# State attention and a Mish layer: the first batch's state read moved, one product widened, the start's list written anew

## The chip, the core and the metric

The kernel runs on one core of a Trainium2 chip. The metric is the device time of one execution in microseconds (us). TensorE is called PE below (its weight loads PEld), VectorE DVE, ScalarE ACT, GpSimd POOL; SP is SyncE, which here only issues DMAs. A kernel's time is the median of its runs; one further run was taken with the profiler.

## The reference

```python
def _attn_ref(x, state):            # x (8, 8, 512, 64), state (8, 8, 32, 64)
    scores = scale * np.matmul(x, state.transpose(0, 1, 3, 2))
    ...                             # softmax over the last axis: a
    xread = np.matmul(a, state)
    scores2 = scale * np.matmul(state, x.transpose(0, 1, 3, 2))
    ...                             # softmax over the last axis: a2
    sread = np.matmul(a2, x)
    return np.concatenate([xread, sread], axis=2).astype(np.float32)

def _moe_ref(x, w_in, w_out):       # w_in (512, 2048), w_out (2048, 512), 64-bit floats
    h = x @ w_in
    sp = np.where(h > 20.0, h, np.log1p(np.exp(np.minimum(h, 20.0))))
    g = h * np.tanh(sp)
    return (g @ w_out).astype(np.float32)
```

The 8 heads of 64 are laid side by side, so each of the 8 batches gives 512 tokens from `xread` and 32 from `sread`, all of width 512, and these go through the second function.

## The kernel before

**Tokens of x.** For the tokens of `xread`, the kernel doesn't form `a @ state` but `ph = a (state w_in)`: `swp` is the small product of a batch's state (block by block, `bd`) with a slice of `w_in`, and `ph` that of the softmax weights with it. Then g = Mish(ph) and `acc` += g w_out. A precise product takes three fast ones of high and low parts: `ah swh`, `al swh`, `ah swl` for `ph`, and likewise `gh`, `gl` with the two parts of `wo` for `acc`. The work goes in 8 groups j of 256 columns of `w_in`: gemm1 makes `ph` in two banks, gemm2 adds to the four banks of `acc` (one for each 128 tokens).

**State tokens.** They need `sread` of a batch: the transposed softmax weights `e2T` times x give `srp`, scaled into `srd`. Its transpose in high and low parts is `srT`; it has room for all 8 batches, 256 tokens. These go through gemm1_s (`ph_s`) and gemm2 (`acc_s`) once, ahead of batch 7.

**The start.** Weights arrive as 64-bit words in 8 pieces of `w_in` (`wir`) and 8 of `w_out` (`wor`). Each is scaled (steps h), rounded (c on ACT, d on DVE) and joined (j) to 32-bit floats; w_out then gets its parts (`wh`, `lo`). This and the whole of batch 0 run by a list of step names (lines 803 to 814). `InOrder` (line 58) keeps DVE and ACT to the order of the list and PE and the loads to that of the program. Capital letters are steps of batch 1, whose softmax is done in the same list.

**The rest.** After the list, loops over the batches (`key` 1 to 7) and j (0 to 7) write the steps, and the scheduler orders DVE and ACT. The product `second` of a group stands one or two groups behind its `first`. All DMAs but two are issued by SP, in one order.

**What the change touches.** Of batch 0's state read, the list has: `mm` and `ee` (softmax over the tokens), `et` (`e2_transposed`, line 393: PE transposes `e` into `e2p`, ACT copies it to `e2T`), `sr` (`sread`, line 494) and `rt` (`sreadT`, line 513: one PE transpose `srTp`, then two parts). In later batches `e2_turned` (line 380) takes the place of `et`: DVE transposes blocks of 32 into `u`, and 16 DMAs put them in order in `e2T`; `soft2` (the softmax) and this step, `turn`, of batch 1 stand at key 1, j = 0 and 1. x_0 lies in the place of the last piece of `w_out`, `wo7`. gemm1_s stands at line 620. The loads are written in one line ahead of the list (line 697).

Of the kernel before, what the change touches and what calls it, by code (L numbers as in the profile page):

```python
# [17 lines left out]
P = 128  # L18
# [59 lines left out]
def state_attention_mish_kernel(ctx, tc, x, state, w_in, w_out, out):  # L78
# [39 lines left out]
    srT = [const.tile([P, NC, B * NS], F32R, name=f"srT_{n}") for n in ("h", "l")]  # L118

    def load_x(b):  # L120

        shape = [P, NC, 2, NT * D]
        if b == 0:
            xs = const.tile(shape, F32, tag="wo7", name="x_0")
        else:
            xs = pool.tile(shape, F32, tag="x", name=f"x_{b}", bufs=1)
        for c in range(NC):
            last["load"] = nc.sync.dma_start(
                xs[:, c], x[b].rearrange("(c k) (p t) d -> c p k (t d)", k=2, t=NT)[c])
        return xs  # L130
# [152 lines left out]
    def attention(b, sn, xq=None):  # L283
# [16 lines left out]
        def scores_q():  # L300

            pss = [bank(f"sc_{b}_{q}") for q, bank in enumerate((misc, misc, first_bank, first_bank))]
            order = [(k, i, c) for k in range(2) for i in range(2) for c in range(NC)]
            if b == 0:
                order.sort(key=lambda s: s[2])
            for k, i, c in order:
                o = slice(c * NS, (c + 1) * NS)
                for q in range(4):
                    last["PE"] = pe.matmul(
                        pss[q][o, k * P:(k + 1) * P].rearrange("n (t p) -> n t p", t=NT),  # L310
                        bqs[b][quad(q), i, 2 * c + k],
                        xTs[c][quad(q)].rearrange("d (k t i p) -> d k i t p", k=2, t=NT, i=2)[:, k, i],
                        start=(i == 0), stop=(i == 1))
            yield
            scs = pool.tile([P, 2, S], F32, tag="sc", name=f"scs_{b}", bufs=1)
# [64 lines left out]
        def e2_turned():  # L380

            both = pool.tile([P, 2 * NT, P], F32, tag="e2T", name=f"e2T_{b}", bufs=1)
            for kc in range(2):
                e2T[kc] = both[:, kc * NT:(kc + 1) * NT]
            u = pool.tile([P, 2, S], F32, tag="sc", name=f"u_{b}", bufs=1)
            for kc in range(2):
                dve.transpose(u[:, kc], e2s[kc])
            v = u.rearrange("i k (t q n) -> i q (k t) n", t=NT, q=4)
            for c in range(NC):
                for q in range(4):  # L390
                    nc.sync.dma_start(both[quad(q), :, quad(c)], v[quad(c), q])

        def e2_transposed(kc):
            e2 = e2s[kc]
            pt = misc(f"e2p_{b}_{kc}")
            for t in range(NT):
                pe.transpose(pt[:, t * P:(t + 1) * P], e2[:, t * P:(t + 1) * P], ident)
            yield
            if not e2T:
                both = pool.tile([P, 2 * NT, P], F32, tag="e2T", name=f"e2T_{b}", bufs=1)  # L400
                e2T.update({k: both[:, k * NT:(k + 1) * NT] for k in range(2)})
            act.copy(e2T[kc].rearrange("p t n -> p (t n)"), pt)


# [89 lines left out]
        def sread(kc):  # L494

            if b == 0 or kc == 0:
                srd["bank"] = misc(f"srp_{b}_{kc}") if b == 0 else spare(2)(f"srp_{b}")
            pr = srd["bank"][:, :D] if b == 0 else srd["bank"][:, kc * D:(kc + 1) * D]
            for t in range(NT):
                for h4 in range(4):  # L500
# [3 lines left out]
                        e2T[kc][:, t, o],  # L504
# [4 lines left out]
            if kc == 0 and b == 0:  # L509
                srd[0] = pool.tile([P, 2, D], F32, tag="srd", name=f"srd_{b}", bufs=1)  # L510
            dve.tensor_scalar_mul((srds[0][:, b - 1] if b else srd[0])[:, kc], pr, rs2[kc])

        def sreadT():
            pt = misc(f"srTp_{b}")[:, :P]
            pe.transpose(pt, srd[0].rearrange("p k d -> p (k d)"), ident)
            yield
            ptv = pt.rearrange("p (c n) -> p c n", c=NC)
            hi, lo = (t[..., b * NS:(b + 1) * NS] for t in srT)
            act.copy(hi, ptv)
            yield  # L520
            dve.tensor_sub(lo, ptv, as_f32(hi))

        own = dict(
            x=x_transposed, st=lambda _: state_blocks(b, sn) if b else state_blocks_0(sn), sc=lambda _: scores() if b > 1 else scores_q(), tr=soft1_t, ex=soft1_x,
            no=lambda _: soft1_n(), pr=soft1_a, mm=soft2_m, ee=soft2_e, et=e2_transposed, sr=sread,
            rt=lambda _: sreadT(), fill=fill, aT=aT)
# [12 lines left out]
    def sreads_transposed():  # L539
        for bs in (range(1, 5), range(5, B)):  # L540
            pt = first_bank(f"srTp_{bs[0]}")
            for i, b in enumerate(bs):
                pe.transpose(pt[:, i * P:(i + 1) * P], srds[0][:, b - 1].rearrange("p k d -> p (k d)"), ident)
# [45 lines left out]
    def low_g(g, gh, gl):  # L589
        dve.tensor_sub(gl, g, as_f32(gh))  # L590
# [132 lines left out]
    def mish_half(j, k):  # L723
# [5 lines left out]
        dve.tensor_copy(gh[:, k * 512:(k + 1) * 512], g[:, k * 512:(k + 1) * 512])  # L729
# [9 lines left out]
    def high_w_half(o, k):  # L739
        if o not in wo:  # L740
            new_wo(o)
        dve.tensor_copy(wo[o][:, k, 1], wfull[o][:, k])
# [15 lines left out]
    def by_tiles(j):  # L758
# [5 lines left out]
    at0, at1 = attention(0, sn0), attention(1, sn1)  # L764
# [22 lines left out]
        "ga": lambda j: by_tiles_half(j, 0), "gb": lambda j: by_tiles_half(j, 1),  # L787
        "wha": lambda o: high_w_half(o, 0), "whb": lambda o: high_w_half(o, 1),
# [6 lines left out]
        "fill": lambda i: at0["fill"](i, accs[0][NT - 1]), "acc": lambda _: new_accs(0, NT),  # L795
        "next": lambda _: sw_slice(1, 0),
# [41 lines left out]
    srds[0] = pool.tile([P, B - 1, 2, D], F32, tag="wt", name="srds", bufs=1)  # L838
    for key, j in slots:
# [24 lines left out]
        if key == 1 and j == 0:  # L864
            prev["soft2"]()
# [35 lines left out]
        if more and j == 4:  # L901
            with behind("swh", "swl"):
# [45 lines left out]
```

## Time and profile before

| | us |
|---|---|
| median of 3 runs | 650.08 |
| lowest and highest | 649.78, 650.28 |
| the profiled run | 649.78 |
| its span | 648.0 |
| PE busy | 640.3 (99%) |
| DVE busy | 353.0 (54%) |
| ACT busy | 246.9 (38%) |

The span goes from the first to the last thing that the profiler recorded. In the profile every computing instruction has line 70, since `InOrder` issues them all; so rows are told apart by the names of their tiles (`out<-in`). A row of the timeline has the start, the time until the last of its instructions ended, the engine, the operation and the count; as products overlap in the pipeline, their pace is read from one row's start to the next one's.

### The profile page before, as it was taken

How to read it: one execution, taken by the hardware profiler on the slowest of the kernel's cores; microseconds unless marked ns; L12 is line 12 of the kernel's file. 1: busy time of each engine (PE TensorE's matmuls, PEld its weight loads, DVE VectorE, ACT ScalarE, POOL GpSimd, SP SyncE). 2: the span in 40 equal slices, each digit the busy share in tenths (PEclk: the TensorE clock that was granted, in tenths of full speed). 3: DMA queues.
4: the chain of work that ended last, by engine and by line, in shares of the span. 5: the costliest groups of instructions: out<-in, count | busy, mean ns of one | idle time of the engine just before them, and what ended most of it. 6: DMA issues, size and time to landing. Idle time of an engine off the chain costs nothing.

```text
span 648.0 us, 11382 instructions
## 1 busy us (share of the span) xinstructions
PE 640.3 (99%) x4686; PEld 515.9 (80%) x4686; DVE 353.0 (54%) x551; ACT 246.9 (38%) x395; POOL 0.7 (0%) x6
## 2 busy tenths in 40 slices
PE   8899999999999999999999999999999999999997
PEld 6677777787878888787878788787878799878886
DVE  5999994674529363655338262855359254332222
ACT  4987952452226122532226212622236234131110
POOL 0000000000000000000000000000000000000000
PEclk9999999999999999999999999999999999999999
DMA  8986323430134103420234003410112001000001
GB/s 322 411 276 207 47 43 81 105 50 5 45 67 109 19 9 92 104 34 9 71 60 93 8 8 98 107 26 1 66 66 34 1 1 66 1 17 17 1 0 66
DMA packets 112611, 46.04 MB, mean 71 GB/s; under 512 B 93744, under 2 KB 102192, under 8 KB 112560
## 3 DMA queue, kind: packets, MB, share of 16 engines
q1 hardware_dynamic: 112128, 45.12, 26.0%
q8 instruction: 37, 0.61, 0.4%
q10 hardware_dynamic: 432, 0.20, 0.1%
q14 instruction: 14, 0.11, 0.1%
HBM read 32.70 MB, written 8.91 MB: 64 GB/s over the span
## 4 chain that ended last, share of the span: by engine, by line
PE 96%; DMA 2%; ACT 1%; DVE 0%; issue 0%; SPq 0%
PE acc L70 55%; PE ph L70 27%; PE swp L70 5%; PE ph_s L70 4%; PE acc_s L70 3%; DMA wor<-in_moe_w_out_dram 1%; PE srp L70 1%; PE sc L70 1%; DMA x<-in_x_dram 0%; DVE s L70 0%; DVE e L70 0%; ACT L70 0%; ACT wor L70 0%; ACT ah L70 0%; ACT wir L70 0%; PE e2p L70 0%
## 5 line engine op out<-in xcount | busy, mean ns | idle before, releaser
L70 PE MATMUL acc<-wo,gh 128*128 128x512 f32 x1024 | 318.4, 392 | 0.0
L70 PEld LDWEIGHTS acc<-wo,gh 128*128 128x128 f32 x1024 | 190.4, 188 | 46.6 <-issue 7.2
L70 PE MATMUL acc<-wo,gl 128*128 128x512 f32 x512 | 199.4, 389 | 0.0
L70 ACT ACTIVATE g<-ph 128x512 f32<-128x512 f32 x128 | 73.7, 597 | 226.2 <-DVE gl L70 207.0
L70 DVE CAST gh<-g 128x1024 fp32r<-128x1024 f32 (+1 forms) x61 | 41.5, 680 | 134.0 <-PE acc L70 132.1
L70 PEld LDWEIGHTS acc<-wo,gl 128*128 128x128 f32 x512 | 96.1, 188 | 20.4
L70 DVE TENSOR_TENSOR gl<-g,gh 128x1024 fp32r<-128x1024 f32 (+1 forms) x65 | 78.3, 1205 | 4.5
L70 PE MATMUL ph<-ah,swh 128*128 128x512 f32 x256 | 79.4, 392 | 0.2 <-ACT g L70 0.2
L70 PE MATMUL ph<-ah,swl 128*128 128x512 f32 x256 | 78.9, 390 | 0.0
L70 PE MATMUL ph<-al,swh 128*128 128x512 f32 x256 | 78.8, 390 | 0.0
L70 DVE TENSOR_TENSOR swl<-swp,swh 128x512 fp32r<-128x512 f32 (+1 forms) x72 | 41.0, 624 | 48.0 <-ACT swh L70 48.0
L70 ACT ACT_TABLE_LOAD x35 | 44.9, 1283 | 31.1 <-DVE s L70 13.5
L70 PEld LDWEIGHTS ph<-ah,swh 128*128 128x128 f32 x256 | 47.5, 188 | 11.3 <-ACT g L70 0.8
L70 PEld LDWEIGHTS ph<-ah,swl 128*128 128x128 f32 x256 | 48.1, 188 | 10.4 <-DVE swl L70 0.4
L70 PEld LDWEIGHTS ph<-al,swh 128*128 128x128 f32 x256 | 48.0, 188 | 10.4 <-DVE al L70 0.4
L70 ACT CAST swh<-swp 128x512 fp32r<-128x512 f32 (+1 forms) x72 | 34.6, 546 | 29.8 <-PE swp L70 29.7
L70 PE MATMUL swp<-w_in_sb,bd 64*32 64x256 f32 x1024 | 34.9, 381 | 0.0
L70 PEld LDWEIGHTS swp<-w_in_sb,bd 64*32 64x32 f32 x1024 | 19.0, 106 | 11.8 <-issue 5.3
L70 DVE COPY o<-acc 128x512 f32<-128x512 f32 x16 | 11.0, 691 | 31.0 <-PE acc L70 31.0
L70 ACT COPY o<-acc 128x512 f32<-128x512 f32 (+1 forms) x17 | 9.5, 563 | 44.1 <-PE acc L70 44.1
L70 DVE STREAM_TRANSPOSE xT<-xq 128x512 f32<-128x512 f32 x24 | 23.7, 1063 | 0.0
L70 PE MATMUL acc_s<-wo,gh_s 128*128 128x512 f32 x64 | 20.0, 394 | 0.0
(90 smaller groups left out, 453.8 us busy)
## 6 DMA issues: line engine op xcount, KB each, us to landing
x<-in_x_dram SPq DMA_DIRECT2D x32, 256.0 KB, 3.7
wir<-in_moe_w_in_dram SPq DMA_DIRECT2D x16, 512.0 KB, 10.0
wor<-in_moe_w_out_dram SPq DMA_DIRECT2D x16, 512.0 KB, 8.0
xq<-in_x_dram SPq DMA_DIRECT2D x192, 32.0 KB, 2.3
out_dram<-o SPq DMA_DIRECT2D x23, 256.0 KB, 2.4
e2T<-u SPq DMA_DIRECT2D x112, 32.0 KB, 1.9
out_dram<-o SPq DMA_DIRECT2D x32, 64.0 KB, 1.7
sn<-in_state_dram SPq DMA_DIRECT2D x28, 32.0 KB, 2.1
```

Of the source, the lines that this page charges most:

```text
L70: made = method(*args, **kwargs)
```

## The change

1. Batch 0's state read leaves the list. The weights `e` are turned at the list's end by the later batches' step (`tu`: two DVE transposes into `u`, 16 DMAs into `e2T`), x_0 is loaded a second time, and `sread` stands at key 1, j = 1. `sreadT` and `e2_transposed` go; the transposes of the state tokens have all 8 batches. Batch 1's `soft2` and `turn` stand one group later.
2. `e2T` and `u` have another layout, so that each transfer moves 32 rows in pieces of 256 numbers rather than of 32.
3. gemm1_s takes both parts of `srT` in one product of 512 columns with the weights' high part, and one of 256 with their low part; the two halves are added by DVE before Mish.
4. The loads become steps of the list (`ldi`, `ldo`, `lx`), the list is written anew, and some copies can be made by ACT (`Ma`, `Mb`, `Wa`, `Wb`).
5. `soft1` of the later batches gets one more rule of order ("low before").

```diff
-    srT = [const.tile([P, NC, B * NS], F32R, name=f"srT_{n}") for n in ("h", "l")]
+    srT_both = const.tile([P, NC, 2, B * NS], F32R, name="srT")
+    srT = [srT_both[:, :, i] for i in range(2)]
...
-            both = pool.tile([P, 2 * NT, P], F32, tag="e2T", name=f"e2T_{b}", bufs=1)
+            both = pool.tile([P, NC, 2, NT, NS], F32, tag="e2T", name=f"e2T_{b}", bufs=1)
             for kc in range(2):
-                e2T[kc] = both[:, kc * NT:(kc + 1) * NT]
-            u = pool.tile([P, 2, S], F32, tag="sc", name=f"u_{b}", bufs=1)
+                e2T[kc] = both[:, :, kc]
+            u = pool.tile([P, 4, 2, NT * NS], F32, tag="sc" if b else "wt", name=f"u_{b}", bufs=1)
             for kc in range(2):
-                dve.transpose(u[:, kc], e2s[kc])
-            v = u.rearrange("i k (t q n) -> i q (k t) n", t=NT, q=4)
+                dve.transpose(
+                    u[:, :, kc].rearrange("i q (t n) -> i t q n", t=NT),
+                    e2s[kc].rearrange("n (t q p) -> n t q p", t=NT, q=4))
             for c in range(NC):
                 for q in range(4):
-                    nc.sync.dma_start(both[quad(q), :, quad(c)], v[quad(c), q])
+                    nc.sync.dma_start(
+                        both[quad(q), c].rearrange("p k t n -> p (k t n)"), u[quad(c), q].rearrange("i k m -> i (k m)"))
...
-        def sreadT():
...
-        for bs in (range(1, 5), range(5, B)):
+        for bs in (range(4), range(4, B)):
...
     def gemm1_s(j):
 
         g = new_g(f"s_{j}")
-        ph = [ps_h.tile([P, 512], F32, tag="ph", name=f"ph_s_{j}_{r}") for r in range(2)]
         for r in range(2):
             for k in range(2):
                 fc = 4 * j + 2 * r + k
+                ph = (first_bank, misc)[k](f"ph_s_{j}_{r}_{k}")
...
                 for c in range(NC):
-                    for n, (l, i) in enumerate(((hi, 0), (hi, 1), (lo, 0))):
-                        pe.matmul(
-                            ph[r][:, k * 256:(k + 1) * 256], l[:, c], srT[i][:, c],
-                            start=(c == 0 and n == 0), stop=(c == NC - 1 and n == 2))
-        for r in range(2):
-            take_g(g, r, ph[r])
+                    pe.matmul(
+                        ph, hi[:, c], srT_both[:, c].rearrange("p i t -> p (i t)"),
+                        start=(c == 0), stop=(c == NC - 1))
+                for c in range(NC):
+                    pe.matmul(
+                        ph[:, :256], lo[:, c], srT[0][:, c], start=False, stop=(c == NC - 1), skip_group_check=True)
+                to = g[:, (2 * r + k) * 256:(2 * r + k + 1) * 256]
+                act.copy(to, ph[:, 256:])
+                dve.tensor_add(to, to, ph[:, :256])
+                last["mish"] = act.activation(to, to, AF.Mish)
...
-    load(("i", 0), ("o", 0), ("i", 1), ("i", 2), ("o", 1), ("i", 3), ("o", 2), ("i", 4), ("o", 3), ("i", 5))
-    with behind("load"):
-        xss[1], sn1 = load_x(1), load_state(1)
-    load(("o", 4), ("o", 6), ("o", 5), ("i", 6), ("i", 7), ("o", 7))
...
-            st acc st x0 hia0 x1 st x2 x3 dia0 jia0 sc sc sc sc tr0 sc tr1 coa0 dib0 fill2 tr0
...
+            st st x1 x0 ldi0 ldo0 hia0 x2 acc ldi1 ldi2 x3 st sc ldo1 fill2 dia0 ldo3 sc ldi3 jia0 sc tr0 ldo2
...
+            ja7 g5 n6 PR0 ja7 lg6 PR1 p7 PR1 PR0 next g6 g6 next g6 lo7 PR1 g6 PR0 next tu n7 n7 lg7
...
+    xss[0] = pool.tile([P, NC, 2, NT * D], F32, tag="raw", name="x_0_again", bufs=2)
+    with behind("load"):
+        load_x(0, xss[0])
...
-        if key == 1 and j == 0:
-            prev["soft2"]()
...
         if key == 1 and j == 1:
-            with behind("mish"):
-                prev["turn"]()
+            beside += [at0["sr"](k) for k in range(2)]
...
+        if key == 1 and j == 1:
+            with behind("swl"):
+                prev["soft2"]()
+        if key == 1 and j == 2:
+            with behind("mish"):
+                prev["turn"]()
```

How the instructions stand at three places, by the order in which each engine gets them. A row has the line, the operation, the tiles written and read, a shape and a count; numbers in a name tell batch, group or part, a last number only one tile from another.

**SP, from the last load of a weight to the first results.** Before:

```order
L191 DMA wor_153<-in_moe_w_out_dram 128x1024 x2
L224 DMA sn_1130<-in_state_dram 32x8x32 x4
L141 DMA xq_1097<-in_x_dram 32x8x32 x32
L391 DMA e2T_1222<-u_1223 32x8x32 x16
L684 DMA out_dram<-o_0_1179 32x512 x4
L684 DMA out_dram<-o_1_1191 32x512 x4
```

After:

```order
L182 DMA wir_400<-in_moe_w_in_dram 128x2x512 x2
L227 DMA sn_1095<-in_state_dram 32x8x32 x4
L144 DMA xq_1062<-in_x_dram 32x8x32 x32
L131 DMA x_again<-in_x_dram 128x2x256 x4
L395 DMA e2T_1035<-u_1036 32x256 x16
L671 DMA out_dram<-o_0_1132 32x512 x4
L671 DMA out_dram<-o_1_1144 32x512 x4
L227 DMA sn_1835<-in_state_dram 32x8x32 x4
L671 DMA out_dram<-o_2_1243 32x512 x4
L671 DMA out_dram<-o_3_1255 32x512 x4
L395 DMA e2T_1326<-u_1327 32x256 x16
```

Before, the first 16 `e2T` are batch 1's and stand ahead of batch 0's results; now those in this place are batch 0's, behind the second load of x_0, and batch 1's follow the four stores of results.

**PE, around batch 0's `srp`.** Before, in the list, between groups 3 and 2:

```order
L70 MATMUL ph_3_1_574<-al_344,swh_3_562 128x512 x2
L70 MATMUL ph_3_1_574<-ah_343,swl_3_563 128x512 x2
L70 MATMUL e2p_1_589<-ident,e_0_1_519 128x128 x4
L70 MATMUL srp_0_605<-x_79,e2T_570 32x64 x16
L70 MATMUL acc_0_179<-wo_546,gh_2_596 128x512 x2
```

After, in batch 1 (`acc` with `gh_7` is batch 0's last group, `ph_2` batch 1's third):

```order
L70 MATMUL swp_2_0_1175<-w_in_sb,bd_604 32x256
L70 MATMUL swp_2_1_1176<-w_in_sb,bd_604 32x256
L70 MATMUL srp_1193<-x_again,e2T_1035 32x64 x32
L70 MATMUL acc_2_132<-wo_961,gh_7_1058 128x512 x2
L70 MATMUL acc_2_132<-wo_961,gl_7_1059 128x512
```

Both halves of `srp` (16 rows each) now stand together, behind a slice of `swp`, and `e2p` is gone.

**PE, the first block of the state tokens.** Before, three such rows stand four times for each block; here are the last three of the first block and the first three of the second:

```order
L70 MATMUL ph_s_0_5113<-srT_h,wh_0_0_5115 128x256
L70 MATMUL ph_s_0_5113<-srT_l,wh_0_0_5115 128x256
L70 MATMUL ph_s_0_5113<-srT_h,wl_0_0_5116 128x256
L70 MATMUL ph_s_0_5113<-srT_h,wh_0_1_5131 128x256
L70 MATMUL ph_s_0_5113<-srT_l,wh_0_1_5131 128x256
L70 MATMUL ph_s_0_5113<-srT_h,wl_0_1_5132 128x256
```

After, the first two blocks whole, behind the last row of batch 6 ahead of them:

```order
L70 MATMUL acc_3_4588<-wo_918,gl_6_4949 128x512
L70 MATMUL ph_s_0_0_5119<-srT,wh_0_0_5120 128x512 x4
L70 MATMUL ph_s_0_0_5119<-srT,wl_0_0_5121 128x256 x4
L70 MATMUL ph_s_0_1_5135<-srT,wh_0_1_5136 128x512 x4
L70 MATMUL ph_s_0_1_5135<-srT,wl_0_1_5137 128x256 x4
```

Products with `srT_h` and `srT_l` by the same weights became one, and each block has a bank of its own.

More of the change, by code (lines that the diff above doesn't have):

```diff
@@ L116, in state_attention_mish_kernel, with load_x @@
     wo = {}
-    srT = [const.tile([P, NC, B * NS], F32R, name=f"srT_{n}") for n in ("h", "l")]
-    def load_x(b):
+    srT_both = const.tile([P, NC, 2, B * NS], F32R, name="srT")
+    srT = [srT_both[:, :, i] for i in range(2)]
+    def load_x(b, xs=None):
         shape = [P, NC, 2, NT * D]
-        if b == 0:
+        if xs is not None:
+            pass
+        elif b == 0:
             xs = const.tile(shape, F32, tag="wo7", name="x_0")
@@ L314, in scores_q @@
             yield
-            scs = pool.tile([P, 2, S], F32, tag="sc", name=f"scs_{b}", bufs=1)
+            scs = pool.tile([P, 2, S], F32, tag="sc" if b else "e2T", name=f"scs_{b}", bufs=1)
             for kc in range(2):
@@ L494, in sread @@
         def sread(kc):
-            if b == 0 or kc == 0:
-                srd["bank"] = misc(f"srp_{b}_{kc}") if b == 0 else spare(2)(f"srp_{b}")
-            pr = srd["bank"][:, :D] if b == 0 else srd["bank"][:, kc * D:(kc + 1) * D]
+            if kc == 0:
+                srd["bank"] = first_bank(f"srp_{b}")
+            pr = srd["bank"][:, kc * D:(kc + 1) * D]
             for t in range(NT):
@@ L503, in sread @@
                         pr[o],
-                        e2T[kc][:, t, o],
+                        e2T[kc][:, h4, t],
                         xss[b][:, h4, kc, t * D:(t + 1) * D],
@@ L508, in sread @@
             yield
-            if kc == 0 and b == 0:
-                srd[0] = pool.tile([P, 2, D], F32, tag="srd", name=f"srd_{b}", bufs=1)
-            dve.tensor_scalar_mul((srds[0][:, b - 1] if b else srd[0])[:, kc], pr, rs2[kc])
-        def sreadT():
[L514 to L521, printed above, removed]
+            if not srds:
+                srds[0] = pool.tile([P, B, 2, D], F32, tag="wt", name="srds", bufs=1)
+            dve.tensor_scalar_mul(srds[0][:, b, kc], pr, rs2[kc])
         own = dict(
-            x=x_transposed, st=lambda _: state_blocks(b, sn) if b else state_blocks_0(sn), sc=lambda _: scores() if b > 1 else scores_q(), tr=soft1_t, ex=soft1_x,
-            no=lambda _: soft1_n(), pr=soft1_a, mm=soft2_m, ee=soft2_e, et=e2_transposed, sr=sread,
-            rt=lambda _: sreadT(), fill=fill, aT=aT)
+            x=x_transposed, st=lambda _: state_blocks(b, sn() if b == 1 else sn) if b else state_blocks_0(sn), sc=lambda _: scores() if b > 1 else scores_q(), tr=soft1_t, ex=soft1_x,
+            no=lambda _: soft1_n(), pr=soft1_a, mm=soft2_m, ee=soft2_e, sr=sread, tu=lambda _: e2_turned(), fill=fill, aT=aT)
         def soft2():
@@ L539, in sreads_transposed @@
     def sreads_transposed():
-        for bs in (range(1, 5), range(5, B)):
+        for bs in (range(4), range(4, B)):
             pt = first_bank(f"srTp_{bs[0]}")
             for i, b in enumerate(bs):
-                pe.transpose(pt[:, i * P:(i + 1) * P], srds[0][:, b - 1].rearrange("p k d -> p (k d)"), ident)
+                pe.transpose(pt[:, i * P:(i + 1) * P], srds[0][:, b].rearrange("p k d -> p (k d)"), ident)
             i = pt[:, :len(bs) * P].rearrange("p (b c n) -> p b c n", c=NC, n=NS)
@@ L589, in low_g @@
     def low_g(g, gh, gl):
-        dve.tensor_sub(gl, g, as_f32(gh))
+        last["low before"] = last.get("low")
+        last["low"] = dve.tensor_sub(gl, g, as_f32(gh))
     def new_g(key):
@@ L695, in load, with load_batch_1 @@
                     rawo[i] = load_w_out(i)
-    load(("i", 0), ("o", 0), ("i", 1), ("i", 2), ("o", 1), ("i", 3), ("o", 2), ("i", 4), ("o", 3), ("i", 5))
-    with behind("load"):
-        xss[1], sn1 = load_x(1), load_state(1)
-    load(("o", 4), ("o", 6), ("o", 5), ("i", 6), ("i", 7), ("o", 7))
+    def load_batch_1():
+        with behind("load"):
+            xss[1] = load_x(1)
+            sns[1] = load_state(1)
+    sns = {}
     pending = []
@@ L721, in first_half, with mish_half @@
         phs[j][k] = gemm1(0, j, aTs[0], sw, (k,))[0]
-    def mish_half(j, k):
+    def mish_half(j, k, copy=None):
         if k == 0:
@@ L728, in mish_half @@
         yield
-        dve.tensor_copy(gh[:, k * 512:(k + 1) * 512], g[:, k * 512:(k + 1) * 512])
+        (copy or dve.tensor_copy)(gh[:, k * 512:(k + 1) * 512], g[:, k * 512:(k + 1) * 512])
     def low_half(j, k):
@@ L737, in by_tiles_half, with high_w_half @@
             yield
-    def high_w_half(o, k):
+    def high_w_half(o, k, copy=None):
         if o not in wo:
             new_wo(o)
-        dve.tensor_copy(wo[o][:, k, 1], wfull[o][:, k])
+        (copy or dve.tensor_copy)(wo[o][:, k, 1], wfull[o][:, k])
     def low_w_half(o, k):
@@ L763, in state_attention_mish_kernel @@
     sw, aTs, phs, gs = {}, {}, {}, {}
-    at0, at1 = attention(0, sn0), attention(1, sn1)
+    at0, at1 = attention(0, sn0), attention(1, lambda: sns[1])
     aTs[0], aTs[1] = at0["aT"], at1["aT"]
@@ L787, in state_attention_mish_kernel @@
         "ga": lambda j: by_tiles_half(j, 0), "gb": lambda j: by_tiles_half(j, 1),
+        "Ma": lambda j: mish_half(j, 0, act.copy), "Mb": lambda j: mish_half(j, 1, act.copy),
+        "Wa": lambda o: high_w_half(o, 0, act.copy), "Wb": lambda o: high_w_half(o, 1, act.copy),
         "wha": lambda o: high_w_half(o, 0), "whb": lambda o: high_w_half(o, 1),
@@ L795, in state_attention_mish_kernel @@
         "fill": lambda i: at0["fill"](i, accs[0][NT - 1]), "acc": lambda _: new_accs(0, NT),
+        "ldi": lambda i: load(("i", i)), "ldo": lambda o: load(("o", o)), "lx": lambda _: load_batch_1(),
         "next": lambda _: sw_slice(1, 0),
@@ L837, in state_attention_mish_kernel @@
     own = at1
-    srds[0] = pool.tile([P, B - 1, 2, D], F32, tag="wt", name="srds", bufs=1)
+    xss[0] = pool.tile([P, NC, 2, NT * D], F32, tag="raw", name="x_0_again", bufs=2)
+    with behind("load"):
+        load_x(0, xss[0])
     for key, j in slots:
@@ L901, in state_attention_mish_kernel @@
         if more and j == 4:
-            with behind("swh", "swl"):
+            with behind("low before", "swh", "swl"):
                 own["soft1"]()
```

29 lines of the change are left out of this document (8 added, 21 removed).

## The prediction, made before the run

> **What bounds the kernel now.** I read the page's busy shares first, then its chain, then the windows of the start.
>
> ```profile
> span 648.0 us, 11382 instructions
> ...
> PE 640.3 (99%) x4686; PEld 515.9 (80%) x4686; DVE 353.0 (54%) x551; ACT 246.9 (38%) x395; POOL 0.7 (0%) x6
> ```
>
> Its chain, by engine:
>
> ```profile
> PE 96%; DMA 2%; ACT 1%; DVE 0%; issue 0%; SPq 0%
> ```
>
> Two windows of 10 us from the list of steps (length, then PE, PEld, DVE, ACT and POOL busy, the granted clock, DMA):
>
> ```profile
> 50.00:60.00 10.00, 10.00 (x86) 7.45 (x85) 8.61 (x15) 8.20 (x10) 0.00 (x0) 1.00 0.69 248
> ...
> 80.00:90.00 10.00, 10.00 (x72) 7.42 (x71) 9.96 (x19) 8.31 (x14) 0.00 (x0) 1.00 0.25 40
> ```
>
> PE is busy for 99% of the span and makes 96% of the chain, so from about 20 us on a PE instruction that goes is time that goes, provided that nobody else is late in its place. The windows show who could be: at the list's end DVE is full as well (9.96 of 10 us), with air before (8.61). The clock is 1.00 in both.
>
> Two rows of the chain give PE's own pace:
>
> ```profile
> 525.00 11.51 PE ph_s L70 x96
> ...
> 586.86 5.44 PE acc L70 x24
> ```
>
> A 512-column product takes 5.44/24 = 226.7 ns from start to start, a 256-column one 11.51/96 = 119.9 ns. A pair of 512 columns is thus 0.45; what the distance between two starts has above that is a wait or a switch of operands.
>
> **A: the start of the list.** Products of the first 20 us wait for loads and for batch 0's softmax; DVE sets the end of that, by `al`.
>
> ```profile
> 19.54 1.29 DVE L70 TENSOR_TENSOR al<-at,ah 128x512 fp32r<-128x512 f32 x2
> ```
>
> What PE does behind it:
>
> ```profile
> 20.18 0.73 PE L70 MATMUL ph<-ah,swh 128*128 128x512 f32 x2
> ...
> 26.62 0.66 PE L70 MATMUL swp<-w_in_sb,bd 64*32 64x256 f32 x16
> ```
>
> `al` is ready at 20.8. From 20.18 to the third slice's `swp` at 26.62 stand 24 products of 512 columns, 24 x 226.7 ns = 5.44 us, in 6.44: 1.00 us of waits, which is all that a better order can take here. In the new list DVE has the same chain up to `al` (two state blocks, transposes, joins of the first two pieces of w_in), so I leave its time at 20.5. Laying the new DVE order behind it with the durations of the same shapes in this trace, the join of w_in's third piece, which `swp` needs, ends at 26.07, so `swp` stands at about 26.15: **-0.47**. Bounds: -1.0 (all waits gone) and +0.6 (`al` as much later as one of its two instructions, 0.65).
>
> **B: the state read leaves the list.** PE's rows where it stood, each group with the start behind it. The first transposition of the weights `e`:
>
> ```profile
> 41.78 0.60 PE L70 MATMUL e2p<-ident,e 128*128 128x128 f32 x4
> 42.13 0.71 PE L70 MATMUL ph<-ah,swh 128*128 128x512 f32 x2
> 42.68 0.62 PE L70 MATMUL ph<-al,swh 128*128 128x512 f32 x2
> ```
>
> The second one, with the first half of the products `srp`:
>
> ```profile
> 44.97 0.60 PE L70 MATMUL e2p<-ident,e 128*128 128x128 f32 x4
> 45.50 0.65 PE L70 MATMUL srp<-x,e2T 128*32 128x64 f32 x32
> 46.08 0.72 PE L70 MATMUL acc<-wo,gh 128*128 128x512 f32 x2
> 46.65 0.40 PE L70 MATMUL acc<-wo,gl 128*128 128x512 f32 x1
> ```
>
> The second half:
>
> ```profile
> 50.89 0.39 PE L70 MATMUL acc<-wo,gl 128*128 128x512 f32 x1
> 51.21 0.65 PE L70 MATMUL srp<-x,e2T 128*32 128x64 f32 x32
> 51.79 0.73 PE L70 MATMUL ph<-ah,swh 128*128 128x512 f32 x2
> 52.37 0.62 PE L70 MATMUL ph<-al,swh 128*128 128x512 f32 x2
> ```
>
> And the transposition of the result:
>
> ```profile
> 60.92 0.27 PE L70 MATMUL srTp<-ident,srd 128*128 128x128 f32 x1
> 60.95 0.71 PE L70 MATMUL ph<-ah,swh 128*128 128x512 f32 x2
> 61.50 0.62 PE L70 MATMUL ph<-al,swh 128*128 128x512 f32 x2
> ```
>
> Each place costs from the end of the pace before it to the second start behind it, less one pair: 42.68 - 41.78 - 0.45 = 0.45; 46.65 - 44.97 - 0.45 = 1.23; 52.37 - (50.89 + 0.23) - 0.45 = 0.80; 61.50 - 60.92 - 0.45 = 0.13. Together **-2.6**. Nothing on PE takes these places but the list's own products, if they are ready.
>
> **C: a wait in the last third product of the list.**
>
> ```profile
> 92.94 0.88 PE L70 MATMUL ph<-ah,swl 128*128 128x512 f32 x2
> 93.67 0.64 PE L70 MATMUL ph<-ah,swh 128*128 128x512 f32 x2
> ```
>
> 0.73 instead of 0.45: PE waits 0.27 for `swl`. In the new list I find this `swl` ready 1.3 us before its product: **-0.27** (bounds 0 and -0.27).
>
> **D, E: the state read beside the second product of batch 1.** The same 64 products stand, for batch 7, here:
>
> ```profile
> 514.63 1.19 PE L70 MATMUL srp<-x,e2T 128*32 128x64 f32 x64
> 515.75 0.73 PE L70 MATMUL acc<-wo,gh 128*128 128x512 f32 x2
> ```
>
> **+1.12**; as there, they follow `swp`, which pays the switch back to 512 columns already. Batch 0's transposition joins the seven others of the state tokens: one more `srTp`, **+0.1** (0.13 above).
>
> **F: the state tokens' first product.** For each of 16 column blocks and 4 slices of the contraction one 512-column product takes the place of two with 256: 64 x (2 x 119.9 - 226.7) = 64 x 13.1 ns = **-0.84**. The Trainium skill ("TensorE: Matmul & The Clock Gate", section "Wait — 56ns, not 53.3ns?") puts the fixed part of a product at about 2.5 ns beside its columns; by it this term would be 64 x 2.5 ns = -0.16. The rows say 13.1 ns; the sum goes by them.
>
> New here are an ACT copy, a DVE addition and a Mish of 256 columns for each block. Not shown at that size; the nearest row, a Mish of 512 columns (its mean is 597 ns):
>
> ```profile
> L70 ACT ACTIVATE g<-ph 128x512 f32<-128x512 f32 x128 | 73.7, 597 | 226.2 <-DVE gl L70 207.0
> ```
>
> A block keeps PE for 4 x (226.7 + 119.9) ns = 1.39 us. If 256 columns cost ACT as much as 512, a block is, with the copy of its 512 weights, 3 x 0.60 = 1.8; at half that for copy and Mish 1.2. Above 1.39 PE would wait, but only in the first 8 blocks, which follow each other (later ones have 5.5 us of second products between): 8 x 0.4 = 3.3 at most, less what four banks hold in store. I take 0, since an elementwise pass goes with its columns, and keep the upper end for the range.
>
> **G: the transfers of e2T.** The queue of SP is one line, and batch 0's 16 transfers are new in it:
>
> ```profile
> 60.56 22.66 SPq L141 DMA_DIRECT2D xq<-in_x_dram  x32
> 85.53 11.43 SPq L391 DMA_DIRECT2D e2T<-u  x16
> 97.36 3.64 SPq L684 DMA_DIRECT2D out_dram<-o  x8
> ```
>
> Four loads of a batch's x, as x_0's second load will be:
>
> ```profile
> 120.93 2.90 SPq L128 DMA_DIRECT2D x<-in_x_dram  x4
> ```
>
> The landing of an e2T transfer after its issue (the page's list of DMA issues: KB, us):
>
> ```profile
> e2T<-u SPq DMA_DIRECT2D x112, 32.0 KB, 1.9
> ```
>
> What the transfers wait for on DVE, and then the row ahead of the product that will read batch 0's:
>
> ```profile
> 84.21 1.29 DVE L70 STREAM_TRANSPOSE u<-e 128x512 f32<-128x512 f32 x2
> ```
>
> ```profile
> 100.62 1.09 PE L70 MATMUL swp<-w_in_sb,bd 64*32 64x256 f32 x32
> ```
>
> Behind `xq` (60.6 + 22.7 = 83.2) come the 4 loads of x_0 (2.9, to 86.1). `u` takes two instructions of 0.6 on DVE (in the new list it ends at 86.8 by my walk; its output is strided now, and at twice the time it would end at 88.0, still within what follows). The pieces grow from 128 B to 1 KB. How long such an issue takes no row shows: 0.71 (11.43/16, same tensor, small pieces) or 0.455 (3.64/8, `out`, pieces of 2 KB in the same 32 rows). I take 0.455, the nearer in shape: 86.8 + 7.3 + 1.9 to land = 96.0. The `srp` that reads it follows `swp` of 100.62, 3.3 earlier by A to C: 97.3 + 1.0 = 98.3. In time. For batch 1 the issues start behind the stores of its predecessor's last two tiles, at about 105.9 by the same walk, and end 105.9 + 7.3 + 1.9 = 115.1; its `srp` stands near 116 (102.3, where batch 0's last product ends, plus 60 products of 226.7 ns). Margin 0.9, or 0.3 if the products ahead lie as tightly as my walk puts them: **+0.2**, bounds 0 and 5.0 (below).
>
> **Sum.** -0.47 - 2.6 - 0.27 + 1.12 + 0.1 - 0.84 + 0.2 = -2.8 on a span of 648.0: 645.2. The profiled run took 649.78, its span and 1.78 around it; so 647.0 for a run like this one. The median of the three runs shown is 650.08, 0.3 above it, which gives 647.3. I say **647.2**.
>
> What the rest rests on: DVE must not be late. By the walk the tightest places in the list are the fourth slice's `swl` (0.5 us ahead of PE) and, at the end, the last `gl` (1.7 ahead).
>
> **Rivals.**
>
> 1. *The pieces don't matter.* If an e2T transfer keeps its 0.71, batch 0's ends at 86.8 + 11.4 + 1.9 = 100.1, 1.8 after `srp` could start; the stores behind it move with PE, so batch 1's ends at 105.9 + 1.8 + 13.3 = 121.0 against 117.8: 3.2 more. PE waits 5.0 (G's upper end) in place of 0.2: **652.0**, slower than before. At 0.65 the two waits are 0.8 and 2.2, the gain is gone (650.2), and from about 0.69 on the kernel is slower by over 0.2%. For it: all rows of e2T are near 0.7. Against: `out`, with twice the bytes in fewer pieces, is at 0.455. The Trainium skill ("DMA: Bandwidth & Descriptors", section "Why small descriptors are slow (HBM only)") says that transfers within the SBUF don't suffer from small pieces; by that rule 1 KB pieces gain nothing and this rival is the outcome. No row of before tells, since e2T has one form there.
>
> 2. *DVE becomes the bound of the list.* PE's part of the list gets 3.3 us shorter while DVE gains two transposes (1.2). In the window 80 to 90 DVE is at 9.96 and at 92.94 PE waits for it. If DVE ends no earlier, PE waits for all it saved and for `u`: 3.3 + 1.2 = 4.5 back, **651.6**; at half of it 649.4. Against: 1.4 us of DVE's window 50 to 60 are idle, which an order with earlier loads can fill, and some copies of the list go to ACT (8.2 to 8.3 of 10 in the two windows).
>
> 3. *F is worth 0.16 only*: **647.9**.
>
> 4. *The list's order buys nothing*, it only moves its waits: A and C are 0, **648.0**.
>
> **How the numbers follow.** A measurement of this kernel can tell 0.2% (1.3 us) from no change: faster means below 648.8, slower above 651.4. Forecast 0.58, rivals 3 and 4 0.05 each: faster 0.68. Rival 1 has 0.12, of which 0.07 at full price; rival 2 0.20, of which 0.05 at full price and 0.15 in part: slower 0.12, same 0.20. The low end of the range is the sum with all of A's waits gone and no wait at e2T, less the 0.3 between the runs: 646.3; the high end takes in the partial cases of both rivals, 650.9.
>
> **What would show it.** In the changed profile: `swp` of the third slice near 26.1; no `e2p` and no `srp` before 90; the list's last `swl` without a wait; e2T's 16 issues in 7 to 8 us instead of 11.4; `srp` of batch 0 near 98 without idle time before it, that of batch 1 near 116; ph_s in the chain at about 1.39 per block. An idle PE before either `srp` is rival 1, waits for `swl`, `gl` or w_in's joins between 30 and 95 are rival 2. What would make it wrong beyond these: loads in the new order landing after the step that joins them.

## The result and the profile after

| | us | runs |
|---|---|---|
| before, median | 649.6 (649.19 to 650.36) | 12 |
| after, median | 652.87 (650.43 to 655.35) | 12 |
| ratio, 95% interval | 1.0051 (1.0037 to 1.0065) | |
| profiled run after, its span | 655.35, 653.4 | |

The kernel became slower, by 0.5%, and its runs lie four times as far apart. They go with the granted clock (the share of PE's full speed that the chip allowed): its mean is 0.999 to 1.0 in the runs with 650.43 and 651.28, 0.995 to 0.997 from 651.97 to 653.85, 0.994 from 654.14 up; the profiled run of before has 1.0. The profile after shows a run with 0.994.

The page's head and chain after:

```profile
span 653.4 us, 11302 instructions
...
PE 89%; SPq 7%; DMA 1%; issue 1%; DVE 1%; ACT 0%; DVEq 0%
```

SP's queue (`SPq`), 0% of the chain before, is 7% of it now. Windows in which PE's busy time (the number behind the length) or its clock (third number from the right) is not full:

```profile
18.00:19.00 1.00, 1.00 (x6) 1.00 (x5) 1.00 (x3) 0.76 (x2) 0.00 (x0) 0.50 1.06 434
...
21.00:22.00 1.00, 1.00 (x18) 0.50 (x18) 0.84 (x2) 0.09 (x1) 0.00 (x0) 0.86 0.99 381
...
116.00:120.00 4.00, 2.91 (x17) 1.95 (x15) 0.00 (x0) 0.42 (x1) 0.00 (x0) 1.00 0.18 49
120.00:124.00 4.00, 1.00 (x58) 1.03 (x58) 0.00 (x0) 0.00 (x0) 0.00 (x0) 0.96 0.21 44
124.00:126.00 2.00, 2.00 (x49) 1.00 (x49) 0.48 (x2) 0.00 (x0) 0.00 (x0) 0.50 0.34 52
```

Two places: the start, and 118 to 127, where PE idles and then works at half its clock. In this profile the clock has two values: cut into windows of 1 us it is 0.50 from 17.9 to 21.3 and from 123.7 to 127.1, 3.4 us each time, and 1.00 around. PE's timeline at the start (start, length, instructions, idle time before and who ended it):

```profile
16.75 0.65 PE L70 MATMUL at<-ident,e 128*128 128x128 f32 x4 [1.51 <-DVE e L70]
17.64 0.95 PE L70 MATMUL at<-ident,e 128*128 128x128 f32 x4 [0.23 <-DVE e L70]
18.38 2.77 PE L70 MATMUL acc<-xT 128*128 128x128 f32 x12
21.08 0.72 PE L70 MATMUL swp<-w_in_sb,bd 64*32 64x256 f32 x16
...
28.01 0.67 PE L70 MATMUL swp<-w_in_sb,bd 64*32 64x256 f32 x16
```

`acc<-xT` are the filling products that keep PE busy; the six of them (each shows as two instructions, as e7's 20 below show as 40) take 2.77 us at the half clock and 1.50 at the full one (e2 below). The next slice's `swp` comes later by that, and with it `swl`, `g` and the whole list. The third slice's `swp` stands at 28.01, before at 26.62. Both places of `srp`:

```profile
99.92 0.31 PE L70 MATMUL srp<-x_again,e2T 128*32 128x64 f32 x6
100.79 1.05 PE L70 MATMUL srp<-x_again,e2T 128*32 128x64 f32 x58 [0.56 <-issue]
101.78 0.73 PE L70 MATMUL acc<-wo,gh 128*128 128x512 f32 x2
...
118.33 0.31 PE L70 MATMUL srp<-x,e2T 128*32 128x64 f32 x4
119.48 0.27 PE L70 MATMUL srp<-x,e2T 128*32 128x64 f32 x2 [0.84 <-DMA e2T<-u]
123.00 1.29 PE L70 MATMUL srp<-x,e2T 128*32 128x64 f32 x58 [3.25 <-DMA e2T<-u]
124.22 1.96 PE L70 MATMUL sc<-xT,bd 64*32 64x256 f32 x32
125.93 2.49 PE L70 MATMUL swp<-w_in_sb,bd 64*32 64x256 f32 x64
128.34 0.73 PE L70 MATMUL acc<-wo,gh 128*128 128x512 f32 x2
```

Each begins with the heads whose pieces of `e2T` are there and waits for the rest: 0.56 and 4.1 us. The scores and `swp` behind the second wait take 1.71 and 2.41 instead of 0.89 and 2.11. What SP does until then:

```profile
62.94 22.75 SPq L144 DMA_DIRECT2D xq<-in_x_dram  x32
85.79 2.07 SPq L131 DMA_DIRECT2D x_again<-in_x_dram  x4
89.39 10.08 SPq L395 DMA_DIRECT2D e2T<-u  x16
99.56 5.23 SPq L671 DMA_DIRECT2D out_dram<-o  x8
104.89 1.88 SPq L227 DMA_DIRECT2D sn<-in_state_dram  x4
106.87 3.67 SPq L671 DMA_DIRECT2D out_dram<-o  x8
110.65 10.02 SPq L395 DMA_DIRECT2D e2T<-u  x16
```

From 62.9 to 120.7 the queue waits for 1.5 us only, for `u` at 89.2. An issue of `e2T` takes 10.08/16 = 0.63 us, not 0.455. The last of batch 1 is issued at 120.7, and PE goes on at 123.0. A sum over such a row can hold one slow issue. Here are the shortest, the median and the longest (ns) of nine stores, the first eight of which are the row at 99.56:

```profile
L671 SPq DMA_DIRECT2D out_dram<-o x9: 392/429/1785, 99.6 to 106.9; - x9
```

One store takes 1.79 us instead of 0.43, and the queue behind it is 1.4 us later for that. What it waits for the profile doesn't say. And so it is with the 11.43 us for 16 issues of `e2T` in the kernel before, from which the prediction had its 0.71:

```profile
L391 SPq DMA_DIRECT2D e2T<-u x16: 608/609/1604, 85.5 to 96.4; - x16
```

Without the slow one, the other 15 stand (11.43 - 1.60)/15 = 0.655 us apart.

The same instructions in both profiles show where the 5.4 us of the span come from:

| up to | before | after | change in this stretch | forecast |
|---|---|---|---|---|
| `swp`, third slice | 26.62 | 28.01 | +1.39 | -0.47 |
| `swp` ahead of batch 0's `srp` | 100.62 | 98.90 | -3.11 | -2.87 |
| `acc` behind that `srp` | 101.64 | 101.78 | +1.86 | +1.12 |
| `acc` behind batch 1's `srp`, scores, `swp` | 122.21 | 128.34 | +5.99 | +0.2 |
| first `ph_s` | 524.84 | 531.02 | +0.05 | +0.1 |
| end | 648.0 | 653.4 | -0.78 | -0.84 |

The rows add up to the 5.4 us of this one run, which had both falls of the clock, and not to the 3.3 us between the medians.

### The profile page after: what moved, and what is told of

The parts are those of the page before. It is cut to its first block, busy times and chain, and to the rows that moved or that the text cites. A ratio compares the mean times of both kernels' runs of the same rounds, so it can differ in the third digit from the quotient of the medians.

```text
span 653.4 us, 11302 instructions
## 1 busy us (share of the span) xinstructions
PE 641.6 (98%) x4614; PEld 514.3 (79%) x4614; DVE 357.6 (55%) x563; ACT 256.5 (39%) x421; POOL 0.7 (0%) x6
## 4 chain that ended last, share of the span: by engine, by line
PE 89%; SPq 7%; DMA 1%; issue 1%; DVE 1%; ACT 0%; DVEq 0%
PE acc L70 50%; PE ph L70 24%; PE swp L70 4%; PE ph_s L70 3%; PE acc_s L70 3%; SPq L144 3%; SPq L395 3%; PE sc L70 2%; SPq L671 1%; PE srp L70 1%; DMA sn<-in_state_dram 0%; DMA e2T<-u 0%; DMA xq<-in_x_dram 0%; PE scT L70 0%; SPq L227 0%
## 5 line engine op out<-in xcount | busy, mean ns | idle before, releaser
L70 DVE TENSOR_SCALAR srds<-srp,rs 128x64 f32<-128x64 f32 x16 | 3.8, 278 | 32.3 <-PE srp L70 32.3
```

The source lines that it names most:

```text
L70: made = method(*args, **kwargs)
```

## The experiments

Theory: what the change saves is there, but (1) SP's queue brings batch 1's `e2T` too late, (2) PE's idle time lets the clock fall, here and in the start. Rivals: DVE's order is late; the clock falls at random; the pieces of `e2T` do it. What the new rule of order for `soft1` is worth was not tried. Each run's "before" is of the same chip.

| run | median | clock, mean of each run | before | ratio (95%) |
|---|---|---|---|---|
| e1 fill early | 653.56 | 0.994 to 0.997 | 649.83 | 1.0066 (1.0050 to 1.0081) |
| e2 stores behind | 650.22 | 0.997 to 1.0 | 649.83 | 1.0006 (0.9996 to 1.0016) |
| e3 small pieces | 654.34 | 0.995 to 0.996 | 649.83 | 1.0070 (1.0053 to 1.0086) |
| e4 wide product alone | 649.0 | 0.997 to 1.0 | 649.83 | 0.9991 (0.9982 to 0.9999) |
| e5 = e1 + e2 | 648.72 | 0.999, 1.0 | 649.46 | 0.9989 (0.9980 to 0.9997) |
| e6 = e5, reads later | 648.5 | 0.999, 1.0 | 649.46 | 0.9980 (0.9971 to 0.9988) |
| e7 bridge the wait | 652.69 | 0.996 to 1.0 | 649.46 | 1.0052 (1.0036 to 1.0067) |
| e9 = e1 again | 653.99 | 0.994 to 0.997 | 650.08 | 1.0057 (1.0045 to 1.0068) |
| e10 = e9 + bridge | 652.39 | 0.999, 1.0 | 650.08 | 1.0035 (1.0024 to 1.0047) |
| e11 before, late fill | 652.03 | 0.994 to 0.999 | 650.08 | 1.0033 (1.0017 to 1.0050) |
| e12 = e6, other bank | 648.29 | 0.999, 1.0 | 650.08 | 0.9973 (0.9962 to 0.9984) |

e8 (below) holds transfers alone, so its time is not compared.

### The start

```diff
-            dob0 jib0 sw0 hib1 no no jia1
+            dob0 jib0 sw0 fill6 hib1 no no jia1
```

> The kernel after, with six more filling products on PE between the first slice's swp and the transposition of batch 0's softmax weights (they fill the 1.5 us in which PE idles at 15.2). Theory (clock): the start loses its time because PE's idle stretch from 15.2 to 18.4 lets the granted clock fall to 0.68-0.79 until 22; with the gap filled the clock stays at 1.00 there, the third slice's swp stands at 26.1 to 26.6 instead of 28.0, the list's last products come 1.4 to 1.9 earlier and the run takes 1.4 to 1.9 us less than the kernel after in its runs with the clock drop (about 651 in the median). Rival (order): the new order of DVE and the loads is what is late; then the clock is 1.00 but swp of the third slice stays at 27.6 or later and the time changes by less than 0.5.

The clock is 1.00 up to 110 us and the third slice's `swp` stands at 25.49, 2.5 earlier than in the profile after. Not all of that is the clock: from the first `at` to this `swp` pass 11.26 us after and 9.29 here, and the rest, 0.55, lies ahead of `at`, where the clock of both was 1.00. Its profiled run is 1.8 us shorter than that of the kernel after (653.56, 655.35), as the theory had it. The median is not (about 651 was expected, 653.56 came): all six runs show 0.994 to 0.997, while the kernel after has two of twelve without a fall. In the profile the clock falls behind the wait for batch 1's `e2T`, which no edit here touches, and stays at 0.50 for 6.8 us (118.8 to 125.7), twice as long as there in the profile after; the time at half clock is the same in both. Why, these runs don't tell; that the start alone saves time is not shown by them.

What this profile does show is the queue without the late start: batch 0's 16 transfers begin at 86.85, as the prediction had it, batch 1's at 108.00, and PE still waits 3.8 us at batch 1's `srp` (1.51 and 2.32). Two slow issues, 1.75 us for a store and 1.41 for a transfer, are part of that.

The counterpart, in the kernel before:

```diff
-            ... jib0 fill6 ex1 sw0 fill2 cia1 ... pr0 cob0 fill2 jib1
+            ... jib0 ex1 sw0 cia1 ... pr0 cob0 fill6 fill2 fill2 jib1
```

> The kernel before, with eight of the filling products of its start, which stand ahead of and behind the first slice's swp, moved behind the transposition of the softmax weights, as the new list has them. Theory (it is the place of the filling products that lets the clock fall in the new list): half of the runs or more show 0.997 and are 1.5 to 2 us longer; the median is 650.5 to 651.5. Rival (the clock in the start falls for another reason, for instance the order of the loads): all runs stay at 0.999 to 1.0 and the time at that of the kernel before.

Six of eight runs show 0.994 to 0.997, and the median is 1.95 us above before, 0.5 more than the theory had. Windows of its profile (the clock is 0.50 from 16.2 to 23.0), and PE's timeline in it:

```profile
17.00:18.00 1.00, 0.45 (x2) 0.46 (x3) 1.00 (x3) 1.00 (x2) 0.00 (x0) 0.50 1.03 420
...
22.00:23.00 1.00, 1.00 (x7) 1.00 (x6) 1.00 (x3) 0.00 (x0) 0.00 (x0) 0.50 1.02 406
```

```profile
17.55 1.97 PE L70 MATMUL at<-ident,e 128*128 128x128 f32 x8 [2.15 <-DVE e L70]
```

The loads and DVE's order are those of before; only the filling products moved. So their place is a cause of the fall, and the rival's loads are not needed for it. Their time in the new place costs little by itself: the two runs without a fall took 650.18 and 650.72. And the old place lowers the odds without ruling the fall out: e4, which has the start of before, shows it in its profile (0.50 from 18 to 21, behind a pause of 1.51 us), in one of 11 runs.

### The queue

```diff
-                    for to, part in pieces:
-                        last["store"] = nc.sync.dma_start(to, part)
+                    with behind(*(["turn"] if key == 0 and t > 1 else [])):
+                        for to, part in pieces:
+                            last["store"] = nc.sync.dma_start(to, part)
```

Here `turn` is the last of batch 1's 16 transfers; batch 1's `soft2` and `turn` are written ahead of `second` at key 1, j = 1.

> The kernel after, with batch 0's last two tiles of results stored behind batch 1's 16 e2T transfers instead of ahead of them. Theory (SP's queue): the transfers then start when u is ready (107.4 instead of 110.65), land near 119.4, and PE waits under 1.5 us at batch 1's srp instead of 4.1; if the clock's fall to 0.5 behind it comes from that idle time, it goes too (1.9 more). Together 2.8 to 5 us less than the kernel after: 648 to 650. Rival (something else than the queue is late, the transpose u or the softmax of batch 1): the wait at srp stays over 3 us and the time within 1 us of the kernel after.

SP and PE in its profile:

```profile
105.10 10.03 SPq L395 DMA_DIRECT2D e2T<-u  x16
115.17 4.77 SPq L672 DMA_DIRECT2D out_dram<-o  x8
```

```profile
116.06 1.51 PE L70 MATMUL srp<-x,e2T 128*32 128x64 f32 x64
117.50 1.09 PE L70 MATMUL sc<-xT,bd 64*32 64x256 f32 x32
```

The transfers go out at 105.1; `srp` takes 0.5 us more than without a wait, and the scores follow at full clock. The median is 650.2; the four runs with 0.999 or 1.0 took 648.3 to 649.0, the eight others, with 0.997, took 649.8 to 651.3. That PE waits less follows the theory. Since this edit also writes `soft2` and `turn` one group earlier, the rival (`u` or the softmax late) is met by the kernel after itself: there the last transposition into `u` starts at 106.6 and takes 0.7 us, so `u` is ready at 107.3, and the transfers go out at 110.65.

Both edits together:

> The edits of the runs with the early filling products and with the stores behind e2T together. Theory: two things cost time in the kernel after, the granted clock's fall in the start (in some of its runs) and batch 1's e2T behind the stores; each edit takes away one, so no run shows a mean clock under 0.998, and the time is that of the best runs of the stores edit alone, 648.3 to 649.0. Rival (the clock falls at random, whatever PE's idle time): part of the runs still have 0.997 and the median stays at 650 or above.

All 12 runs at 0.999 or 1.0, 648.1 to 649.6, median 648.72: close to the theory's numbers. With both pauses filled or shortened the clock fell in none of 12 runs, while with the second alone shortened it fell in 8 of 12 (e2) and with the first alone filled in 6 of 6 (e1); so it is not random whatever PE does. It also follows, though no profile shows it, that e2's slower runs had their fall in the start, where alone the two kernels differ.

### What the wait costs beside itself

```diff
+                for _ in range(20 if b == 1 else 0):
+                    pe.matmul(srd["bank"][:, :P], ident, ident, start=True, stop=True)
```

> The kernel after, with 20 filling products (some 0.2 us each) into srp's bank ahead of batch 1's srp, so that PE is busy while it waits for e2T. Theory (clock): the wait for e2T still ends near 123, but the clock stays at 1.00, the scores and the slices of swp behind it take 0.9 and 2.0 us instead of 1.7 and 2.4, and the time is 1 to 2.5 us less than the kernel after; clock 0.997 or more. Rival: these products are slow behind the wait for another reason; then time and pace stay as in the kernel after.

The pace is as the theory had it (`swp` 2.10, before 2.11; clock 1.00 in the profile), the time is not: 652.69, about that of the kernel after. Two of the six runs still show 0.996 and 0.997, most likely by a fall in the start, which this edit leaves as it was. The filling products took 4.6 us and `srp` began right behind them, so whether they held it back can't be seen. Undecided; so a pair was run with the start mended and fewer products (17):

> The kernel with the early filling products once more, as the neighbour of the next run on the same chip: 653 to 654, every run at a clock of 0.994 to 0.997, since its wait for e2T at batch 1's srp lasts over 4 us.

> The same with 17 filling products ahead of batch 1's srp (3.9 of the 4.8 us for which PE waits there). Theory (the wait for e2T costs twice, once as idle time and once by the clock that falls behind it): the wait stays, the clock is 0.999 or 1.0 in all runs, and the time is 1.5 to 2.5 us less than its neighbour's. Rival (the clock's part is small): within 0.7 us of its neighbour.

PE behind the wait without the bridge (e9) and with it (e10):

```profile
121.44 1.89 PE L70 MATMUL srp<-x,e2T 128*32 128x64 f32 x58 [2.31 <-DMA e2T<-u]
123.25 1.96 PE L70 MATMUL sc<-xT,bd 64*32 64x256 f32 x32
124.96 2.58 PE L70 MATMUL swp<-w_in_sb,bd 64*32 64x256 f32 x64
127.47 0.73 PE L70 MATMUL acc<-wo,gh 128*128 128x512 f32 x2
```

```profile
122.37 1.05 PE L70 MATMUL srp<-x,e2T 128*32 128x64 f32 x58 [0.70 <-DMA e2T<-u]
123.36 1.09 PE L70 MATMUL sc<-xT,bd 64*32 64x256 f32 x32
124.24 2.18 PE L70 MATMUL swp<-w_in_sb,bd 64*32 64x256 f32 x64
126.35 0.72 PE L70 MATMUL acc<-wo,gh 128*128 128x512 f32 x2
```

From the last part of `srp` to `acc` 6.03 us without, 3.98 with. The medians differ by 1.6 us (653.99, 652.39; the ranges of both overlap): that is the clock's part. The wait itself stayed: with the bridge too, `srp` ends its wait 12.3 us after the transfers begin (110.10 to 122.37), without it 12.2 (109.25 to 121.44).

### The transfers

```diff
-                    nc.sync.dma_start(
-                        both[quad(q), c].rearrange("p k t n -> p (k t n)"), u[quad(c), q].rearrange("i k m -> i (k m)"))
+                    nc.sync.dma_start(both[quad(q), :, quad(c)], v[quad(c), q])
```

> The kernel after, with the layout of e2T and u of the kernel before (pieces of 128 B instead of 1 KB). Theory (the pieces hardly matter): an issue takes 0.65 to 0.70 instead of 0.63, batch 0's transfers end 0.5 to 1 us later and so do batch 1's, and the time is 0.5 to 2.5 us above the kernel after. Rival (the pieces matter as the prediction had it, and something else slowed the transfers): an issue takes over 0.75, and the time grows by over 4 us.

An issue takes 10.45/16 = 0.65, and the median is 1.5 us above that of the kernel after, with four runs and on another chip; the pieces are a small part.

> Only transfers, all else is left out: 16 each, issued by SP, of 32 rows within the SBUF (1 KB pieces to other rows, 1 KB to the same rows, 128 B pieces, 512 B pieces), from the device memory (1 KB and 128 B pieces), and to it (1 KB and 2 KB pieces). If the size of the pieces sets SP's time for an issue, those of 128 B take over 0.6 and those of 1 KB under 0.5 everywhere; if it is where the data comes from and goes to, transfers within the SBUF take about 0.6 at any size of piece and those to the device memory 0.43 to 0.46.

SP's timeline of its one run, groups of 16 in the order named (`turned` is the change's form, `spread` has pieces of 128 B; the last row holds both stores, 1 and 2 KB):

```profile
3.02 10.10 SPq L48 DMA_DIRECT2D turned<-src  x16
13.16 10.08 SPq L51 DMA_DIRECT2D same_rows<-src  x16
23.29 10.47 SPq L59 DMA_DIRECT2D spread<-src  x16
33.80 10.10 SPq L64 DMA_DIRECT2D half_size<-src  x16
...
49.60 10.38 SPq L70 DMA_DIRECT2D from_dram_small<-in_x_dram  x16
60.03 15.09 SPq L84 DMA_DIRECT2D out_dram<-src  x32
```

Within the SBUF an issue costs 0.63 to 0.65 whatever the pieces, to the device memory 15.09/32 = 0.47; from it in pieces of 128 B 0.65. From it in pieces of 1 KB the issue itself takes 0.42 us in the median, as to it; in pieces of 128 B 0.61. So neither answer holds whole: for these transfers of 32 rows the way sets the price, and for loads the pieces count too.

### The wide product, and a better order

> The kernel before, with only the state tokens' first product changed (512 columns with the weights' high part). By the rows of before, 64 x 13.1 ns = 0.84 us less; by the fixed part of 2.5 ns that the page states, 0.16 less; if ACT's new passes hold PE up, up to 3.3 more. In the kernel after a block takes 1.40 us by its profile, 1.44 before: 0.6 less here, so 648.9 to 649.1 beside 649.6, clock 1.00.

-0.83 us by the medians, -0.6 by the ratio, whose interval reaches from -0.06 to -1.2. The chain of its profile has for the first eight blocks, which took 11.51 us before:

```profile
525.89 11.20 PE ph_s L70 x64
```

A block is 1.40 us, as in the kernel after. ACT's three passes for it are 0.62 (copy of the weights), 0.37 (copy) and 0.42 (Mish) in the kernel after, 1.41 in all: they only just fit.

> The same, and batch 0's srp behind the last products of batch 0, batch 1's srp behind batch 2's scores. Theory: the two waits for e2T that are left, 0.55 and 0.5 us, are covered by these products: 1.0 less than without, 647.3 to 648. Rival: a product behind needs the bank that srp then holds (ph has two) and the wait moves there: no change, or up to 1 us more.

Only 0.2 us in the medians: both waits for `e2T` are gone, but the second half of `ph` stands 0.8 us late; the rival puts that down to the bank that `srp` holds. With `misc` in place of `first_bank` for batch 0:

> The run with the reads later, and batch 0's srp in a bank of the other pool. There ph's second half waited 0.8 us for the bank until DVE had scaled srp; with a bank that nobody wants then, this is gone: 0.7 to 0.8 less, a ratio of 0.9965 to 0.9975 to the kernel before. If the next product waits for something else (swl, gl), no change.

The 0.8 us are gone from its profile, so it was the bank. 0.9973 is the lowest ratio here, and the time is below that of both kernels; from e6 it can't be told apart (0.9980, intervals that overlap, another chip). In its profile batch 1's `srp` still waits 0.2 and the `swp` behind it takes 0.5 us more than before.

## Why the prediction was wrong

- **G is the step that failed**: "I take 0.455, the nearer in shape". The shape was `out`'s, the way was not: within the SBUF an issue is 0.63 us in the profile and alone (e8). The waits are 0.56 + 4.1 us instead of 0.2. For batch 1 the price counts twice, since its 16 issues stand behind the 16 of batch 0: with 0.63 the queue itself is late, and the start that the prediction took from PE's results (105.9) became 110.65. The late list and one slow store issue are part of this; but in e1, whose list is not late, the wait is still 3.8 us. By estimate, 32 issues at 0.455 instead of 0.63 take 5.6 us out of the queue ahead of the read, more than the wait, while the slow issues make 1.4 us of it (after) or 2 (e1). The two runs of the kernel after without a fall of the clock took 650.43 and 651.28, 3.2 and 4.1 us above the forecast, near the 4.5 by which G was too small. The rest up to the median goes with the clock.
- **The other price was misread too.** 0.71 is the mean of 15 issues at 0.655 and one of 1.60. The trace of before thus had the price of this tensor within 0.03 of what came.
- **Rival 1** named this mechanism (a full price at each issue makes both reads wait) and got 0.12, since I weighed a row of the same shape above the rows of the same tensor. That its 5.0 us of waits and 652.0 us came near (4.7, 652.87) is in part luck: they rest on 0.71. At 0.65 its own line has waits of 0.8 and 2.2 us and 650.2; it let the stores move with PE and saw neither the full queue nor the clock. Its reason holds nearly: pieces of 128 B cost 0.65, of 1 KB 0.63. The Trainium skill ("DMA: Bandwidth & Descriptors", section "Why small descriptors are slow (HBM only)") says that transfers within the SBUF don't suffer from small pieces. It speaks of bandwidth; for SP's time of an issue, which counted here, the trace agrees, 0.65 against 0.63.
- **The clock was in no term.** I read 1.00 in two windows and took it for given. Behind the wait it cost 1.6 us (e9, e10) and in the start about 2 (e11).
- **A** came to +1.39 in the profile, and 1.5 us of that are the clock: from the first `at` to the third slice's `swp` pass 11.26 us, in e2, at full clock, 9.73. The term itself stays open. In nine profiles with a full clock there, this `swp` stands between 25.49 (e1) and 27.49 (e3), before at 26.62: the start moves between runs by more than the forecast 0.47.
- **B, C** were right: -3.11 against -2.87, no `e2p` or `srp` in the list, the last `swl` in time. **D, E**: the stretch of D is +1.86, of which 0.56 are the wait, so 1.3 for 1.12; E's stretch is +0.05 for 0.1. **F**: -0.63 by the chain's rows (23.01 to 22.38 us for all blocks), -0.6 to -0.8 by time in e4, instead of -0.84. So rival 3 (0.16 only) fell.
- **Rival 2** fell: from 28 to 99 us the profile after has no wait on PE, and the list took less than forecast.
- Small slips: 650.2 in rival 1 should be 650.0 and 651.6 in rival 2 651.7 by their own sums, and `al`, ready at 20.8, is taken at 20.5. None bears on the outcome.

With both faults mended the sign of the sum comes out (e5 and e12 are faster than before), the size does not: -0.7 us (e5) and -1.8 (e12) against -2.8. In the profile of e12 the missing part stands in one stretch, from the list's last `swp` to the second products behind batch 1's `swp`: +2.4 us against before where the forecast has +1.3; the other stretches come to -4.0 for -4.1.

## What to carry to other kernels

Price an issue by a row of the same way (within the SBUF, to or from the device memory), by the median issue and not by the row's sum, which can hold a slow one. Add up a queue from its last pause to the issue that somebody waits for: if it is full, every issue put in moves all behind it. Where a change takes products away or moves them, look for the places where PE then idles for more than a microsecond. The products behind may run at half the clock for 3.4 or 6.8 us, in some runs only; here that added 1.6 us to a wait of some 4. A few filling products in the pause kept the clock up in all runs (in the start of e5, in both places of e10).

## What was not expected of the hardware

- The granted clock fell to 0.50 in the start though PE's longest pause was 1.5 us (after) or 2.15 us (e11), with other work around it. The Trainium skill ("TensorE: Matmul & The Clock Gate", section "What's actually happening") lets the clock halve after an idle window of about 3.4 us; the half agrees (0.50 from 124 to 126), but the pause did not have to be a whole window.
- Each fall lasts 3.4 us (after, twice; e3, e4) or 6.8 us (e1, e9, e11). That gives the means of the runs: half the clock for 3.4 of 650 us is 0.26%, so by this estimate 0.997 is one such stretch and 0.995 two; the profiled runs of e3 and e4 have 0.996 and 0.997, those of after, e1, e9 and e11 0.994 to 0.995.
- The length of the pause doesn't decide. In the start, pauses of 1.48 (before), 0.95 (e2) and 1.65 us (e3) left the clock at 1.00, and 1.51 (after), 1.51 (e4) and 2.15 us (e11) did not. The same kernel shows a fall in some runs only: 8 of 12 (e2), 6 of 8 (e11). The kernel before, run beside the experiments 61 times, had a mean clock of 0.997 in 3. What decides, these runs leave open.
- SP's time for an issue depends on the way: 0.63 us within the SBUF for 32 rows of 512 B or 1 KB, 0.47 to the device memory (e8). Now and then an issue takes 1 to 2 us, with no wait that the profile names (1.60 before, 1.79 after).
